# Product 7 of block 0 as seven quarter products in a two-level feed-forward kernel

## The chip, the cores and the metric

The kernel runs on one core of a Trainium2 chip. The metric is the device time of one execution in microseconds (us); the kernel before was given as 337.72 us (median of 3 runs, 337.43 to 338.76). A ratio below is the mean time of one kernel's fast runs over the mean of the other's fast runs of the same rounds on the same chip, so it is not quite the ratio of the medians quoted beside it. It stands with its 95% interval.

The profile names the engines PE (TensorE matmuls), PEld (TensorE weight loads), DVE (VectorE), ACT (ScalarE), POOL (GpSimd) and SP or SPq (SyncE, which issues the transfers here). L978 is line 978 of that kernel's source.

## The reference

```python
def reference(x, w1, b1, w2, b2):          # x: 1 x 2048 x 1024, w1: 1024 x 3584, w2: 3584 x 1024, all bf16
    y = _layernorm(x, axis=-1)
    h = _gelu(jnp.einsum("bsd,df->bsf", y, w1) + b1)
    return jnp.einsum("bsf,fd->bsd", h, w2) + b2
```

## The kernel before

The 2048 rows are two blocks of 1024. In each block the first matmul (L767 and others) makes h, the second multiplies h by w2. The second is split into seven half-size products, numbered 1 to 7 and run in the order 1, 5, 2, 6, 7, 3, 4, whose operands are sums of halves made by VectorE. Each of the seven can be done in two ways. A *plain* product is 4 x 14 matmuls of 512 columns. An *inner* product is split once more, into seven quarter products of 14 matmuls of 256 columns, at the price of further sums (w2 inner sums iT, h inner sums iS) and more evictions. In the kernel before, block 0 does products 6 and 7 plain and the other five inner.

```python
INNER = ((1, 5, 2, 3, 4), SEQ2)          # block 0, block 1
...
def plain(p, a, b, banks_, first, deps):
    for t in range(TH):                  # 4 row tiles
        fn = [(lambda e, k=k, t=t: e.matmul(ps[:, banks_[t].k, :], lhsT=a[0][:, k, t * P:(t + 1) * P],
               rhs=b[0][:, k, :], ...), a[1][k] + b[1][k]) for k in range(NU)]        # NU = 14
...
def inner(p, a, Yo, xb, war, O=None, ...):
    s1 = tt(1, X["21"], X["22"], ALU.add, 5)           # the four h inner sums, VectorE
    s2 = tt(2, s1, X["11"], ALU.subtract, 6)
    s3 = tt(3, X["11"], X["21"], ALU.subtract, 7)
    s4 = tt(4, X["12"], s2, ALU.subtract, 3)
    ...                                                # seven sub-products of 14 matmuls of 256 columns
    sd = copy(lambda: bank_q(c2), lambda: quart(g, 0, 0), (ok[11], subs[1]), ...)      # ScalarE: seed
    k1 = copy(kk_q, lambda: bank_q(c0), (subs[1], *gate), ...)                         # ScalarE: first copy
    k5 = dve(lambda e: plus(e, quart(gt, 1, 1), bank_q(c5), quart(g, 1, 1)), ...)      # VectorE: six evictions
```

Product 7 of block 0 is plain, and the next fetch of w1 for block 1 waits for its second row tile:

```python
M7 = plain(7, S3, B[7], hb, False, [(o,) for o in O12])
w1_use[n - 2] = w1_use[n - 2] + [M7[1]]
```

The layernorm of block 1's tiles runs during block 0's second matmul. Three one-column steps of it are on GpSimd:

```python
vp = add("POOL", 0.2, lambda e: e.tensor_scalar(out=vpe_sb[:, i:i + 1], in0=st_sb[:, i, 0:1],
         scalar1=1.0 / D, scalar2=LN_EPS, op0=ALU.mult, op1=ALU.add), (a2,), ...)
rs = add("POOL", 0.6, lambda e: e.tensor_tensor(out=rstd_sb[:, i:i + 1], in0=vpe_sb[:, i:i + 1],
         in1=nhalf[:, :], op=ALU.pow), (vp, c_nh), ...)
nb = add("POOL", 0.3, lambda e: e.tensor_tensor(out=st_sb[:, i, 1:2], in0=mv_sb[:, i, 1:2],
         in1=rstd_sb[:, i:i + 1], op=ALU.mult), (rs, a1), ...)
```

A planner in the kernel puts every instruction on its engine's list from a table of tuned priorities. On the chip each engine works through its list in order.

## Time and profile before

| | before |
|---|---|
| median time | 337.72 us |
| TensorE busy | 329.3 us, 98%, 2399 matmuls |
| VectorE, ScalarE, GpSimd busy | 281.3, 173.2, 22.5 us |
| moved by DMA | 89.47 MB |

The prediction below shows the page's lines, the timeline, the windows and the one gap. A busy share says little on a pipelined array, so I read TensorE by a ledger. From the timeline every matmul has a start-to-start distance to the next. I subtract its undisturbed pace, 215.8, 109.2 or 55.8 ns for 512, 256 or 128 columns, and sum three things: the paces themselves ("nominal"), the excess before 25 us ("head") and the excess after it ("holes", those over 40 ns). With 1.04 us before the first matmul and 2.81 us from the start of the last to the end this makes up the span: 1.04 + 325.59 + 6.47 + 0.28 + 2.81 = 336.19 of 336.2 us. The only hole is the one before 122 us.

### The profile page before, as it was taken

The numbers are of one execution on the slowest core, as the hardware profiler recorded it, in microseconds if no ns is written. First come the engines' busy times: TensorE is split into PE (matmuls) and PEld (weight loads), VectorE is DVE, ScalarE is ACT, GpSimd is POOL, SyncE is SP. The second block draws the span as 40 slices with busy tenths as digits, with TensorE's granted clock in tenths as the row PEclk, the third lists the DMA queues.
The fourth block names the chain that finished last, engine by engine and source line by source line (L and its number), as shares of the span: only waits on it lengthen the run. The fifth ranks groups of instructions, "written<-read, shape, count | busy, mean of one in ns | idle before, by whom it ended". The sixth has DMA issues, their size and how long they took to land.

```text
span 336.2 us, 6035 instructions
## 1 busy us (share of the span) xinstructions
PE 329.3 (98%) x2399; PEld 223.3 (66%) x2399; DVE 281.3 (84%) x381; ACT 173.2 (52%) x292; POOL 22.5 (7%) x47
## 2 busy tenths in 40 slices
PE   4999999999999999999999999999999999999996
PEld 4977445445468885547875555544545888888885
DVE  3896789998999999979999888886738879999984
ACT  5675978566786687612113666765676521010200
POOL 2420120000020413200000000000000000000000
PEclk9899999999999999999999999999999999999999
DMA  7896999797868999899859549839971999999103
GB/s 269 257 181 182 355 354 321 247 329 262 279 238 305 353 336 361 227 318 379 320 173 328 181 174 336 288 138 292 351 226 50 386 319 367 333 326 311 65 2 125
DMA packets 80310, 89.47 MB, mean 266 GB/s; under 512 B 15130, under 2 KB 67226, under 8 KB 79770
## 3 DMA queue, kind: packets, MB, share of 16 engines
q1 hardware_dynamic: 80138, 88.95, 81.6%
q8 instruction: 19, 0.31, 0.4%
q10 hardware_dynamic: 144, 0.13, 0.1%
q14 instruction: 9, 0.07, 0.1%
HBM read 61.81 MB, written 24.38 MB: 256 GB/s over the span
## 4 chain that ended last, share of the span: by engine, by line
PE 93%; ACT 3%; POOL 1%; DVE 1%; DMA 1%; issue 0%
PE ps L767 42%; PE ps L1063 34%; PE ps L978 7%; PE ps L619 5%; PE ps L692 5%; DMA x_sb<-in_x_dram 1%; POOL st_sb L488 1%; PE ps L504 1%; ACT t_sb L474 1%; ACT t_sb L469 1%; PE ps L1068 0%; ACT sn_sb L962 0%; ACT ps L962 0%; DVE st_sb L418 0%; ACT x_sb L491 0%
## 5 line engine op out<-in xcount | busy, mean ns | idle before, releaser
L767 PE MATMUL ps<-yw_sb,t_sb 128*128 128x512 f16 x336 | 80.0, 379 | 0.0
L767 PE MATMUL ps<-yw_sb,w_sb 128*128 128x512 f16 x312 | 74.7, 379 | 0.0
L792 ACT ACTIVATE h_sb<-ps,b_sb 128x512 f16<-128x512 f32 x78 | 52.9, 686 | 37.0 <-PE ps L767 32.3
L767 PEld LDWEIGHTS ps<-yw_sb,t_sb 128*128 128x128 f16 x336 | 32.8, 98 | 35.8 <-DVE ps L807 0.2
L767 PEld LDWEIGHTS ps<-yw_sb,w_sb 128*128 128x128 bf16 x312 | 30.3, 98 | 33.2 <-ACT ps L780 0.3
L854 DVE TENSOR_TENSOR h_sb<-h_sb 128x2048 f16<-128x2048 f16 (+2 forms) x36 | 38.6, 1084 | 7.3 <-ACT h_sb L792 5.3
L962 ACT COPY sn_sb<-ps 128x512 f32<-128x512 f32 x27 | 15.5, 583 | 32.9 <-DVE o_sb L942 18.2
L1063 PE MATMUL ps<-w2a_sb,h_sb 128*128 128x256 f16 (+1 forms) x252 | 30.3, 273 | 0.0
L942 DVE TENSOR_TENSOR sn_sb<-ps,sn_sb 128x512 f32<-128x512 f32 x35 | 24.0, 687 | 5.3 <-PE ps L1063 4.6
L1063 PEld LDWEIGHTS ps<-w2a_sb,h_sb 128*128 128x128 f16 x252 | 24.7, 98 | 3.9
L942 DVE TENSOR_TENSOR o_sb<-ps,sn_sb 128x512 bf16<-128x512 f32 (+1 forms) x29 | 19.3, 670 | 6.3 <-PE ps L1063 3.7
L978 PE MATMUL ps<-w2a_sb,h_sb 128*128 128x512 f16 x112 | 24.5, 379 | 0.0
L1063 PE MATMUL ps<-w_sb,t_sb 128*128 128x256 f16 x196 | 23.4, 273 | 0.1
L962 ACT COPY ps<-sn_sb 128x512 f32<-128x512 f32 x12 | 7.1, 589 | 30.3 <-PE ps L1063 24.6
L780 ACT COPY ps<-ps 128x512 f32<-128x512 f32 x26 | 14.9, 577 | 14.6 <-PE ps L767 14.5
L1063 PEld LDWEIGHTS ps<-w_sb,t_sb 128*128 128x128 f16 x196 | 19.0, 98 | 2.7 <-ACT sn_sb L962 0.4
L807 DVE TENSOR_TENSOR ps<-ps,sn_sb 128x512 f32<-128x512 f32 x26 | 17.6, 694 | 3.4 <-PE ps L767 3.3
L792 ACT ACTIVATE h_sb<-sn_sb,b_sb 128x512 f16<-128x512 f32 x26 | 18.5, 717 | 3.7 <-DVE sn_sb L821 2.8
L587 DVE TENSOR_TENSOR t_sb<-w_sb,t_sb 128x1024 f16<-128x1024 bf16 x26 | 17.9, 687 | 2.8 <-PE ps L767 1.6
L978 PEld LDWEIGHTS ps<-w2a_sb,h_sb 128*128 128x128 f16 x112 | 11.0, 98 | 12.8
L821 DVE TENSOR_TENSOR sn_sb<-ps,sn_sb 128x512 f32<-128x512 f32 x20 | 13.6, 686 | 5.1 <-PE ps L767 5.0
L619 PE MATMUL ps<-yw_sb,w_sb 128*128 128x128 f16 x256 | 16.7, 226 | 0.4 <-DVE yw_sb L511 0.4
(125 smaller groups left out, 485.4 us busy)
## 6 DMA issues: line engine op xcount, KB each, us to landing
w_sb<-in_w_dram SPq DMA_DIRECT2D x28, 512.0 KB, 5.6
x_sb<-in_w_dram SPq DMA_DIRECT2D x21, 256.0 KB, 6.0
w_sums<-x_sb SPq DMA_DIRECT2D x21, 256.0 KB, 3.5
w2a_sb<-w_inner_sums SPq DMA_DIRECT2D x12, 448.0 KB, 7.3
x_sb<-in_x_dram SPq DMA_DIRECT2D x15, 256.0 KB, 4.3
w_inner_sums<-w_sb SPq DMA_DIRECT2D x4, 896.0 KB, 8.2
x_sb<-w_sums SPq DMA_DIRECT2D x2, 1792.0 KB, 9.1
w_sb<-w_inner_sums SPq DMA_DIRECT2D x8, 448.0 KB, 6.9
```

Of the source, the lines that this page charges most:

```text
L587: return add("DVE", 0.65, lambda e: e.tensor_tensor(out=tv(k), in0=x0, in1=x1, op=ALU.subtract), [*deps, *war.get(k, ())], prio + 0.5 * k, ...
L619: fn = [(lambda e, b=b, hb=hold[f], f=f, k=k, t=t: e.matmul(ps[:, hb.k, t * P:(t + 1) * P], lhsT=lhs[:, k, f * P:(f + 1) * P], rhs=yop[f"A ...
L692: fn = [(lambda e, k=k, v=v: e.matmul(ps[:, bank[r].k, v * QN:(v + 1) * QN], lhsT=xo()[:, k, v * P:(v + 1) * P], rhs=yv()[:, k, :], start= ...
L767: fn = [(lambda e, k=k: e.matmul(ps[:, hold[p].k, :], lhsT=lhs[:, k, :], rhs=yop[yo][:, k, :], start=(first and k == 0), stop=(k == KH - 1 ...
L780: return e.copy(out=dst, in_=src) if o_.eng == "ACT" else e.tensor_copy(dst, src)
L792: r = h_ok[(s, q, u)] = add("ACT", 0.70, lambda e: e.activation(out=dst, in_=src(), func=ACT.Gelu_apprx_tanh, bias=b1_sb[:, f:f + 1], scal ...
L807: o2 = add("DVE", 0.7, lambda e: e.tensor_tensor(out=b5v(b5), in0=b5v(b0), in1=v5(), op=ALU.add), (P6, *o5), pt[7] - SLOT, f"w6_{nm}", all ...
L854: o = add("DVE", cost2(w * dst.shape[-1]), lambda e, k0=k0, k1=k1: e.tensor_tensor(out=dst[:, k0:k1, :], in0=a[0][:, k0:k1, :], in1=b[0][: ...
L942: plus = lambda e, out, x, y: e.tensor_tensor(out=out, in0=x, in1=y, op=ALU.add)
L962: return act(lambda e: e.copy(out=out(), in_=src()), deps, at - 5, name, **k)
L978: fn = [(lambda e, k=k, t=t: e.matmul(ps[:, banks_[t].k, :], lhsT=a[0][:, k, t * P:(t + 1) * P], rhs=b[0][:, k, :], start=(first and k == ...
L1063: fn = [(lambda e, k=k, j=j: e.matmul(ps[:, bank[r].k, j * HI:(j + 1) * HI], lhsT=x[0][:, k, j * P:(j + 1) * P], rhs=y[0][:, k, :], start= ...
```

## The change

The change makes product 7 of block 0 an inner product too. It forms the w2 inner sums of product 7 on the spot, and stores none of them in block 0 (block 1 forms them again in its first stage, as before). The w2 transfers for block 1's product 1 are released one w1 chunk sooner. Two of the layernorm's one-column steps go from GpSimd to ScalarE, the bias transpose goes to the front, and the whole priority table was tuned anew with the overlap of neighbouring VectorE and ScalarE instructions in the plan. A few smaller edits (a queue term in the plan, extra dependencies that keep the order of some sums and transfers) are not shown. Cut to its core:

```diff
-INNER = ((1, 5, 2, 3, 4), SEQ2)
+INNER = ((1, 5, 2, 7, 3, 4), SEQ2)
 ORDER = {...                                    # all entries replaced
+OVL = {"DVE": 0.08, "ACT": 0.09}
...
-            vp = add("POOL", 0.2, lambda e: e.tensor_scalar(... scalar1=1.0 / D, scalar2=LN_EPS ...
+            vp = add("ACT", 0.2, lambda e: e.activation(out=vpe_sb[:, i:i + 1], in_=st_sb[:, i, 0:1], func=ACT.Identity,
+                                                        bias=epsc[:, :], scale=1.0 / D), (a2, c_eps), ...
-            nb = add("POOL", 0.3, lambda e: e.tensor_tensor(out=st_sb[:, i, 1:2], in0=mv_sb[:, i, 1:2],
+            nb = add("ACT", 0.2, lambda e: e.mul(st_sb[:, i, 1:2], mv_sb[:, i, 1:2], rstd_sb[:, i:i + 1]), (rs, a1), ...
...
-                if s + 1 < NSB:
+                if s + 1 < NSB and p != 7:      # product 7: inner sums not stored
                     keep(0, y13, uniq(t1[1][0], t3[1][0]), (5, 7))
...
-                Yo = {1: fetch(1, hold[1], base1[s] + 0.6 * T_MM1, w1_use[n - 3]), ...
+                Yo = {1: fetch(1, hold[1], base1[s] + 0.5 * T_MM1, w1_use[n - 4]), ...
...
-            M7 = plain(7, S3, B[7], hb, False, [(o,) for o in O12])
-            w1_use[n - 2] = w1_use[n - 2] + [M7[1]]
-            ...                                  # four evictions o22, four copies O3
+            gw, okq, sub7 = inner(7, S3, inner_sums(7, B[7], Y0, war_of(sub2, 2)), X0, war_of(sub2),
+                                  O=(gu, {11: U[1], 12: U[1], 21: U[3], 22: U[3]}), kk=x_sb[:, NT - 1, :].bitcast(F32))
+            w1_use[n - 2] = w1_use[n - 2] + [sub7[5]] + flat(S4)
+            Yo3 = inner_sums(3, B[3], [two(xf), *halves(xf)[3:1:-1]], {}, True)      # product 3's sums into the x buffer
```

## The prediction

> **What bounds the kernel now.** I read four views in this order: the page, TensorE's timeline, the windows by stage, and the timeline around the one gap that TensorE has. The page first (part 1: busy us, share, instructions; part 4: the chain that ended last):
>
> ```profile
> PE 329.3 (98%) x2399; PEld 223.3 (66%) x2399; DVE 281.3 (84%) x381; ACT 173.2 (52%) x292; POOL 22.5 (7%) x47
> ...
> PE 93%; ACT 3%; POOL 1%; DVE 1%; DMA 1%; issue 0%
> ```
>
> TensorE is 98% busy and carries 93% of the chain. Busy time alone proves little, since matmuls overlap, so the pace has to be checked. TensorE's timeline over products 2, 6 and 7 of block 0 (start, length, what):
>
> ```profile
> 126.56 6.21 PE L978 MATMUL ps<-w2a_sb,h_sb 128*128 128x512 f16 x28
> 132.60 1.69 PE L1063 MATMUL ps<-w_sb,h_sb 128*128 128x256 f16 x14
> 134.13 1.69 PE L1063 MATMUL ps<-yw_sb,t_sb 128*128 128x256 bf16 x14
> 135.66 18.29 PE L978 MATMUL ps<-w2a_sb,h_sb 128*128 128x512 f16 x84
> 153.79 1.69 PE L1063 MATMUL ps<-w2a_sb,h_sb 128*128 128x256 bf16 x14
> ```
>
> L978 is a plain product, L1063 an inner one. From start to start, 28 wide matmuls take 132.60 - 126.56 = 6.04 us, 215.7 ns each; 14 narrow ones 134.13 - 132.60 = 1.53 us, 109.3 ns each. The 112 matmuls of L978 are products 6 and 7; 56 of the 84 in the fourth line are product 7. The same reading over the whole timeline finds TensorE at this pace, without a hole, from about 11 us until its last matmul begins at 333.4 us; the only exception is 0.28 us just before 122 us. So the span is the sum of TensorE's matmuls plus a head and a tail.
>
> What could break that is VectorE. Windows by stage (stretch, its length, then busy us and instructions by engine):
>
> ```profile
> 97.00:126.00 29.00, 28.88 (x257) 24.81 (x256) 26.70 (x28) 20.84 (x36) 6.37 (x8) 1.00 0.95 307
> 126.50:153.80 27.30, 27.30 (x144) 13.77 (x142) 24.91 (x30) 12.69 (x22) 5.05 (x9) 1.00 1.01 305
> 153.80:178.80 25.00, 25.00 (x214) 20.85 (x213) 23.40 (x27) 3.92 (x7) 0.00 (x0) 1.00 0.79 280
> 178.80:200.00 21.20, 21.20 (x112) 10.75 (x110) 18.06 (x32) 12.43 (x21) 0.00 (x0) 1.00 0.68 241
> 200.00:258.00 58.00, 58.00 (x305) 29.66 (x304) 41.68 (x59) 38.33 (x64) 0.00 (x0) 1.00 0.72 237
> ```
>
> The third busy number is VectorE. Around product 7 it has only 27.30 - 24.91 = 2.4, then 25.00 - 23.40 = 1.6, then 21.20 - 18.06 = 3.1 us free; from 200 us on it has 16.3 us free. The gap before 122 us (POOL, ACT, the weight load that waits):
>
> ```profile
> 113.97 2.82 POOL L488 TENSOR_TENSOR st_sb<-mv_sb,rstd_sb 128x1 f32<-128x1 f32 x1
> ...
> 116.83 1.24 ACT L491 ACTIVATE x_sb<-x_sb,st_sb,rstd_sb 128x1024 f16<-128x1024 bf16 x1 [2.00 <-POOL st_sb L488]
> 117.98 0.56 ACT L962 COPY sn_sb<-ps 128x512 f32<-128x512 f32 x1
> ...
> 121.96 1.42 PEld L1063 LDWEIGHTS ps<-w_sb,t_sb 128*128 128x128 f16 x14 [0.40 <-ACT sn_sb L962]
> ```
>
> A one-column multiplication took 2.82 us on GpSimd, ACT stood 2.00 us for it in its order, its bank copies came late, and TensorE paid 0.28 us.
>
> **What the Trainium skill says.** "TensorE: Matmul & The Clock Gate", section "Back-to-back issue gap", gives N/2.4 + 2.5 ns for a single warm matmul, 215.8 at N=512 and 109.2 at N=256; the trace's 215.7 and 109.3 agree. The same section calls this too high for streams with weight loads and gives some 131 ns at N=512; this trace does not show that. "VectorE: DVE Perf Modes", section "The perf-mode tier table", has tensor_tensor at 2x on 16-bit SBUF data and at 1x with a PSUM operand. The trace agrees: 1,792 fp16 elements in 1,086 ns (0.61 ns each), 512 fp32 elements with PSUM in 687 ns (1.34 ns each). "SBUF — State Buffer", section "Who interferes with whom", says that a VectorE instruction with two SBUF inputs keeps out a GpSimd one that reads SBUF. L488's eight runs of the same operation lasted 191 to 2,823 ns, which fits that.
>
> **The change part by part.**
>
> TensorE. Product 7 of block 0 loses 56 matmuls at 215.7 ns = 12.08 us and gains 7 sub-products of 14 at 109.3 ns = 10.71 us. That is -1.37 us, all on the path, since TensorE has no holes there.
>
> VectorE, with the step from start to start where instructions follow each other (the timeline shows 1.93 us for 3,584 fp16 elements, 1.00 for 1,792, 0.60 for a 128x512 eviction; the 128x1024 fp32 sum is taken as 1.15 us, its 1.225 less the same overlap). Added: the w2 inner sums 1.93 + 2 x 1.00 = 3.93; the four h inner sums 4.00; six evictions 3.60; two row sums 2.30; together 13.8. Removed: four evictions of the plain product, 2.4. Net +11.4 us. It is not on the path by itself, but it falls where 2.4 + 1.6 + 3.1 = 7.1 us are free.
>
> ACT. Four copies (O3) go and four come (U); seed and first copy of product 7 add 2 x 0.58 us. The two one-column steps of the second layernorm move here from GpSimd, 8 x 2 x 0.2 = 3.2 us by L472's 200 ns. ACT has 14.6 us free in the second window above and 21.1 in the third, so this costs nothing. What it buys is the 0.28 us gap, since ACT no longer stands behind L488; the power on GpSimd (0.55 us) stays.
>
> DMA. Product 7 stores no sums in block 0, and block 1 forms them during its first matmul stage as before, so the traffic stays near 89.5 MB. Product 3's sums move into the x buffer, so they must follow block 1's transposes out of it, and product 7's first copy goes into the place of x tile 7. The earlier fetch of block 1's product 1 moves a transfer for which TensorE does not wait now: nothing.
>
> Head. The bias transpose may slide into TensorE's idle time before 6.8 us; it holds the array 0.13 us now (9.64 to 9.77). I count -0.1.
>
> Sum without any new wait: 337.72 - 1.37 - 0.28 - 0.1 = 335.97 us.
>
> **The rivals.** First, VectorE becomes the bound of the stage. An inner product costs it 3.93 + 4.00 + 3.60 = 11.5 us against 10.7 us on TensorE, so three in a row (7, 3, 4) run it behind, and the plain product 7, which it used to get ahead, is gone. For: 11.4 us more into 7.1 us free leaves 4.3 us to be pushed past 200 us. Against: from there 16.3 us are free, block 1's sums for products 6 and 7 (8.2 us, L1370) can be done later, and TensorE already mixes first-stage products with the end of product 4. If none of the overhang is hidden it is 340.3 us; if half is, 338.1.
>
> Second, a new wait on the transposes. In the trace before, SyncE issues transposes from 103 to 147 us, one landing a median of 5.0 us after issue, and half of those for tiles 4 to 7 must follow the end of product 2 (about 135.7 us). Product 7 would begin near 141.7 and want its first copy by about 144; a transpose of tile 7 issued third after 135.7 at some 1.7 us each lands near 146. That would be up to 2 us of TensorE wait, unless product 2 is brought to an end earlier, which the reordering may do. Alone: 336 to 338 us.
>
> Third, all is hidden: the whole order was tuned anew, with the overlap of VectorE's instructions now in the plan. 336.0 us.
>
> **Range and chances.** I take the third as most likely, with an allowance of 0.6 us for small waits of the first two kinds: 335.97 + 0.6 = 336.6 us. The low end, 335.5, is the clean sum less a noise of 0.5 (the three runs before spread 1.3 us); the high end, 338.8, is the first rival with a third of the overhang hidden and no more. Over 2% faster means under 331.0 us, which would need over 5 us that no part offers: 0.01. Over 2% slower means over 344.5 us, twice the whole overhang: 0.02. Within 2%: 0.97.
>
> **What would show it right or wrong.** Right: L978 at 56 matmuls and L1063 98 more; VectorE's busy time near 281.3 + 11.4 = 292.7 us; no wait on L488; TensorE still at 215.7 and 109.3 ns without holes from 11 us on. Wrong by the first rival: weight loads of L1063 or L767 waiting for VectorE between 140 and 215 us, VectorE without idle there. Wrong by the second: a hole early in product 7 that ends with the first copy on ACT, which waited for a transpose. The prediction fails upward if those holes add to more than 2 us, and downward if the head shrinks by a microsecond, which I do not expect.

## The result, and the profile after

The kernel after took 337.97 us (median of 5, 337.88 to 339.0), the kernel before in the same rounds 338.5 us (median of 5, 337.43 to 338.87): ratio 0.9998, interval 0.9974 to 1.0022. The time lies inside the forecast range, but the forecast said a gain of 1.1 us over 337.72, and none was measured. The page of the kernel after, parts 1 and 4:

```profile
PE 328.9 (98%) x2441; PEld 227.0 (68%) x2441; DVE 290.5 (86%) x392; ACT 178.1 (53%) x310; POOL 17.2 (5%) x32
...
PE 89%; DMA 7%; DVE 3%; SPq 1%; issue 0%; POOL 0%
```

There are 42 more matmuls (98 - 56) and 9.2 us more on VectorE. In the chain ScalarE and GpSimd are gone, and transfers and VectorE have come in. TensorE's timeline over products 6 and 7 (start, length, what):

```profile
131.61 1.69 PE L1086 MATMUL ps<-w_sb,h_sb 128*128 128x256 f16 x14
133.14 9.23 PE L1000 MATMUL ps<-w2a_sb,h_sb 128*128 128x512 f16 x42
142.21 1.69 PE L1086 MATMUL ps<-w2a_sb,h_sb 128*128 128x256 f16 x14
143.74 3.22 PE L1086 MATMUL ps<-w_sb,t_sb 128*128 128x256 f16 x28
...
157.91 1.90 PE L786 MATMUL ps<-yw_sb,w_sb 128*128 128x512 f16 x8 [0.25 <-DMA w_sb<-in_w_dram]
```

The pace is what it was: 14 narrow matmuls in 143.74 - 142.21 = 1.53 us. After product 6 product 7 starts without a hole. The last line shows two things: block 1's first-stage products (L786) now start at 157.9 us inside the second stage of block 0, where the timeline of before has the first of them at 172.13 us, and this one waits for a transfer. ScalarE around the old gap:

```profile
119.41 1.21 ACT L984 COPY ps<-sn_sb 128x512 f32<-128x512 f32 x2
120.55 0.29 ACT L502 ACTIVATE st_sb<-mv_sb,rstd_sb 128x1 f32<-128x1 f32 x1
```

The one-column step takes 0.29 us here and nobody waits for GpSimd; the gap before 122 us is gone. The windows by stage, in the columns of the prediction's table:

```profile
97.00:126.00 29.00, 29.00 (x256) 24.85 (x255) 28.59 (x31) 27.15 (x52) 4.63 (x3) 1.00 0.99 326
126.50:153.80 27.30, 27.30 (x198) 19.12 (x197) 27.24 (x31) 14.09 (x25) 3.12 (x3) 1.00 0.94 292
153.80:178.80 25.00, 24.75 (x202) 19.40 (x200) 24.97 (x30) 4.72 (x9) 0.00 (x0) 1.00 1.07 336
178.80:200.00 21.20, 21.17 (x119) 11.23 (x118) 19.13 (x31) 11.39 (x19) 0.00 (x0) 1.00 0.51 180
```

From 97 to 178.8 us VectorE, the third busy number, has 0.4, 0.06 and 0.03 us free. In these four windows and the next (45.14 against 41.68) it does 10.3 us more than before. TensorE has holes now. Each stands here with the line that causes it: first the one at 41 us with VectorE's lines before it, then the weight fetch for the one at 158 us, then the weight loads that waited at 183 and 194 us:

```profile
40.96 1.25 PE L786 MATMUL ps<-yw_sb,t_sb 128*128 128x512 f16 x5 [0.29 <-DVE sn_sb L804]
...
37.14 0.69 DVE L595 TENSOR_TENSOR t_sb<-w_sb 128x1024 f16<-128x1024 bf16 x1 [0.91 <-DMA w_sb<-in_w_dram]
...
39.62 0.68 DVE L1434 TENSOR_TENSOR dl_sb<-b_sb 128x512 f32<-128x512 bf16 x1
40.22 0.68 DVE L804 TENSOR_TENSOR sn_sb<-ps,sn_sb 128x512 f32<-128x512 f32 x1
...
147.50 0.94 SPq L362 DMA_DIRECT2D w_sb<-in_w_dram  x2
...
183.55 1.41 PEld L786 LDWEIGHTS ps<-yw_sb,t_sb 128*128 128x128 f16 x8 [0.52 <-DVE t_sb L605]
...
194.08 0.79 PEld L711 LDWEIGHTS ps<-sn_sb 128*128 128x128 f16 x8 [0.27 <-DVE sn_sb L667]
```

At 41 us VectorE had stood 0.91 us for w1 chunk 3, then did its list in order, a bias step (L1434) ahead of the sum (L804) that TensorE wanted. At 158 us the weights had been asked for only at 147.50, after the last h sum of product 3 had ended at 146.96, and landed at 157.86. At 183 and 194 us VectorE is simply not yet there. "TensorE: Matmul & The Clock Gate", section "Architectural detail: the array is 16× 32×32, not 1× 128×128", says in the Trainium skill that VectorE and ScalarE take their instructions strictly first in, first out; the trace agrees, the sum of L804 did not pass the waiting one. So an order is as good as a dependency.

The ledger of the two kernels, the repeats included that are told below:

| kernel, profile | nominal | head | holes (where) | span |
|---|---|---|---|---|
| before | 325.59 | 6.47 | 0.28 (122) | 336.20 |
| before, again | 325.59 | 6.64 | 1.52 (115, 198) | 337.62 |
| after | 324.21 | 6.80 | 1.21 (41, 158, 183, 194) | 336.13 |
| after, again | 324.21 | 8.43 | 1.17 (43, 159, 185, 196) | 337.71 |
| after, third | 324.21 | 7.21 | 1.39 (41, 158, 184, 195) | 336.71 |

The nominal sum fell by 325.59 - 324.21 = 1.38 us. In the means of these profiles the holes give back 1.26 - 0.90 = 0.36 and the head 7.48 - 6.56 = 0.92 us. Together that is -0.10 us, and the mean spans differ by -0.06. So the saved matmul time is there, and the question is what holes and head have to do with the change.

### The profile page after: what moved, and what is told of

Its sections match the earlier page's. It is cut to its first block, busy times and chain, and to the rows that moved or that the text cites. A ratio compares the mean times of both kernels' runs of the same rounds, so it can differ in the third digit from the quotient of the medians.

```text
span 336.1 us, 6135 instructions
## 1 busy us (share of the span) xinstructions
PE 328.9 (98%) x2441; PEld 227.0 (68%) x2441; DVE 290.5 (86%) x392; ACT 178.1 (53%) x310; POOL 17.2 (5%) x32
## 2 busy tenths in 40 slices
DMA packets 80278, 89.47 MB, mean 266 GB/s; under 512 B 15098, under 2 KB 67194, under 8 KB 79738
## 4 chain that ended last, share of the span: by engine, by line
PE 89%; DMA 7%; DVE 3%; SPq 1%; issue 0%; POOL 0%
PE ps L786 39%; PE ps L1086 37%; DMA w_sb<-in_w_dram 5%; PE ps L711 5%; PE ps L638 4%; PE ps L1000 4%; DMA x_sb<-in_x_dram 2%; SPq L362 1%; PE ps L518 1%; PE ps L1091 0%; DVE sn_sb L964 0%; DVE st_sb L431 0%; DVE sn_sb L804 0%; DVE h_sb L873 0%; DVE t_sb L595 0%
## 5 line engine op out<-in xcount | busy, mean ns | idle before, releaser
L786 PE MATMUL ps<-yw_sb,t_sb 128*128 128x512 f16 x336 | 80.2, 379 | 0.3 <-DVE sn_sb L804 0.3
L786 PE MATMUL ps<-yw_sb,w_sb 128*128 128x512 f16 x312 | 75.8, 379 | 0.3 <-DMA w_sb<-in_w_dram 0.3
L786 PEld LDWEIGHTS ps<-yw_sb,t_sb 128*128 128x128 f16 x336 | 32.7, 98 | 36.8 <-DVE sn_sb L804 1.0
L786 PEld LDWEIGHTS ps<-yw_sb,w_sb 128*128 128x128 bf16 x312 | 30.2, 98 | 32.7 <-ACT ps L799 0.6
L1086 PE MATMUL ps<-w2a_sb,h_sb 128*128 128x256 f16 (+1 forms) x280 | 33.3, 273 | 0.0
L1086 PEld LDWEIGHTS ps<-w2a_sb,h_sb 128*128 128x128 f16 x280 | 27.4, 98 | 4.0
L964 DVE TENSOR_TENSOR sn_sb<-ps,sn_sb 128x512 f32<-128x512 f32 x40 | 27.2, 686 | 1.6 <-PE ps L1086 1.5
L964 DVE TENSOR_TENSOR o_sb<-ps,sn_sb 128x512 bf16<-128x512 f32 (+1 forms) x25 | 16.6, 666 | 6.1 <-ACT ps L1162 2.9
L873 DVE TENSOR_TENSOR t_sb<-h_sb 128x1792 f16<-128x1792 f16 x16 | 17.3, 1086 | 0.8 <-ACT h_sb L811 0.6
L840 DVE TENSOR_TENSOR sn_sb<-ps,sn_sb 128x512 f32<-128x512 f32 x20 | 13.6, 687 | 4.4 <-PE ps L786 4.4
L638 PEld LDWEIGHTS ps<-yw_sb,w_sb 128*128 128x128 bf16 x256 | 15.5, 101 | 1.7 <-DMA w_sb<-in_w_dram 1.0
```

The costliest lines, as they stand in the source:

```text
L638: fn = [(lambda e, b=b, hb=hold[f], f=f, k=k, t=t: e.matmul(ps[:, hb.k, t * P:(t + 1) * P], lhsT=lhs[:, k, f * P:(f + 1) * P], rhs=yop[f"A ...
L786: fn = [(lambda e, k=k: e.matmul(ps[:, hold[p].k, :], lhsT=lhs[:, k, :], rhs=yop[yo][:, k, :], start=(first and k == 0), stop=(k == KH - 1 ...
L840: c22 = add("DVE", 0.69, lambda e: e.tensor_tensor(out=v5(), in0=b5v(b0), in1=v5(), op=ALU.add), (P7, o2), pt[4] - SLOT, f"c7_{nm}")
L873: o = add("DVE", cost2(w * dst.shape[-1]), lambda e, k0=k0, k1=k1: e.tensor_tensor(out=dst[:, k0:k1, :], in0=a[0][:, k0:k1, :], in1=b[0][: ...
L964: plus = lambda e, out, x, y: e.tensor_tensor(out=out, in0=x, in1=y, op=ALU.add)
L1086: fn = [(lambda e, k=k, j=j: e.matmul(ps[:, bank[r].k, j * HI:(j + 1) * HI], lhsT=x[0][:, k, j * P:(j + 1) * P], rhs=y[0][:, k, :], start= ...
```

## The experiments

The theory at the outset: VectorE's list, full from 97 to 194 us, leaves TensorE waiting in four places, and these holes ate the gain. The rival: noise of the head hides a gain that is there, and the holes have causes unlike each other. In all edits `move(engine, name, to)` takes one instruction out of an engine's finished list and puts it ahead of another (`after=True`: behind it); nothing else changes unless shown.

### The kernel after once more

> The changed kernel once more, for the spread of its TensorE holes. If they belong to the order of its instructions, the trace shows again about 0.45 us near 41 us, 0.4 us near 158 us, 0.2 us near 183.5 us and 0.15 us near 194 us, each within 0.1 us. If they come from the luck of transfers, at least the two that wait for a w1 or x transfer (the head, 158 us) differ by 0.3 us or more or are gone. Time: same as the kernel before within 0.3%.

338.11 us (337.52 to 341.31, 6 runs), ratio 0.9999 (0.9965 to 1.0034). The holes are at the same places with the same sizes (table above); the head is 1.6 us longer than the first time. So the three late holes look like properties of the kernel and the head does not. For the one near 41 us, later runs show that it depends on when a transfer lands.

### Three single changes to the kernel after

bias_late:

```diff
+        move("DVE", "dl", "c7_0_3", after=True)    # L1434 behind the sum of L804
```

> The changed kernel with one swap in VectorE's order: the sum that releases product 4 of unit 3 (c7_0_3) goes ahead of the 0.68 us bias difference (dl). If the hole near 41 us is only that queueing, it goes from 0.45 to under 0.1 us, the rest of the trace shifts 0.4 us earlier, and the time falls by 0.4 us (ratio to the changed kernel 0.9988). If something else bounds TensorE, the hole's time comes back as wider holes later and the span stays at 336.1 us.

The hole at 41 us went; another came at 68 us, from the same kind of cause (VectorE in line behind a weight sum whose transfer had landed late):

```profile
68.24 1.04 PE L786 MATMUL ps<-yw_sb,w_sb 128*128 128x512 f16 x4 [0.33 <-DVE ps L826]
```

The holes are 1.36 us in sum, the time 338.06 us, ratio 0.9986 (0.9965 to 1.0007).

The swap did close the hole: less the head excess of its profile, the first half of w1 chunk 3 landed at 30.3 us here (36.70 - 6.38), as late as in the three profiles of the kernel after (37.12 - 6.80, 38.71 - 8.43, 37.48 - 7.21), which have holes of 0.40 to 0.45 us. But an early landing does the same: at 29.9 us in w1_early the hole is 0.09 us, and at 29.4 us in dve_minus there is none, though neither edit touches this part; in dve_minus there is none at 68 us either. So neither hole is a fixed cost.

w1_early:

```diff
+        o = named["w1_1_0_0"]                       # first half of block 1's first weight chunk
+        o.deps = [d for d in o.deps if d.name != "M75_0" and not d.name.startswith("hS4_0")]
+        move("SP", "w1_1_0_0", "w2_0_B22_0")
```

> The changed kernel with the first half of block 1's first w1 chunk no longer held back for the h sums S4 and for sub-product 5 of product 7, and issued before the two B22 loads (near 140 us in place of 147.5 us). If the hole near 158 us is the late landing of this transfer, it goes from 0.42 us to under 0.05 us and the span falls by 0.4 us. If VectorE is what bounds there, the time returns in wider holes near 183 and 194 us and the span stays.

The fetch went out at 140.66 us in place of 147.50, and the hole at 158 us is gone. But a hole of 0.33 us came five microseconds later, where ScalarE's seed of product 4 is late:

```profile
158.10 1.89 PE L786 MATMUL ps<-yw_sb,w_sb 128*128 128x512 f16 x8
...
163.41 1.70 PE L1086 MATMUL ps<-h_sb 128*128 128x256 f16 x14 [0.17 <-ACT ps L984]
```

The holes at 183 and 194 us did not change (0.19 and 0.15 us), against the rival. Holes 0.82 us, time 338.64 us, ratio 1.0012 (0.998 to 1.0043).

dve_minus, a wrong result (relative error 0.028):

```diff
+        for k, name in enumerate(("iS5_7_0_0", "iS6_7_0_0", "iS7_7_0_0", "iS3_7_0_0")):
+            named[name].fn = lambda e, k=k: e.tensor_tensor(out=tiny[:, k:k + 1], in0=nhalf[:, :], in1=nhalf[:, :],
+                                                            op=ALU.subtract)     # one column each, in place of 1792
```

> Wrong result on purpose: the four h inner sums of product 7 in block 0 (1.0 us each on VectorE) are replaced by one-column operations, so VectorE has 3.7 us less to do between 137 and 149 us. If VectorE's saturation makes the three late holes, S4 ends earlier, w1 is issued some 1 to 3 us earlier, and the holes near 158, 183.5 and 194 us (0.76 us together) all but vanish: span down by 0.6 to 0.8 us, the hole near 41 us unchanged. If they come from transfers or from TensorE's order alone, they stay.

With four of product 7's sums taken away the late holes stayed: 0.47, 0.19 and 0.15 us at 158, 183 and 194. Ratio 0.9988 (0.9963 to 1.0013). VectorE's windows, in the columns of the tables above:

```profile
126.50:153.80 27.30, 27.30 (x198) 19.11 (x196) 23.95 (x32) 14.02 (x25) 1.38 (x2) 1.00 0.95 282
153.80:178.80 25.00, 24.70 (x200) 19.27 (x199) 24.95 (x29) 5.05 (x9) 0.00 (x0) 1.00 1.06 337
```

In the first window VectorE does 3.3 us less (23.95 against 27.24), and spent it, up to 148 us, in waits for ScalarE and TensorE; the fetch of w1 moved only from 147.50 to 146.91 us. In the second it is as full as before. So work taken away ahead of 148 us does not close the late holes. Whether less work after 148 us would, this run does not test.

### The kernel before once more, and one part of the change alone

> The kernel before once more, unchanged, for the noise of the old side. Theory (the saved matmul time is given back in two ways: reproducible holes of TensorE that the old kernel does not have, and a head before 25 us that varies by some 2 us from execution to execution whatever the kernel): the ratio is 1.000 within 0.3%; the profile has the hole of 0.28 us at 122 us again and no hole at 158, 183 or 194 us; its head excess may lie anywhere between 6.3 and 8.5 us. Rival (the old kernel has the same holes at times and its first profile was lucky): holes of over 0.15 us show up between 150 and 200 us here as well.

338.54 us (337.87 to 339.34), ratio 0.9984 (0.9958 to 1.0009). Half the expectation was wrong: the gap before 122 us was absent, and the old kernel had two others:

```profile
115.40 1.70 PE L1063 MATMUL ps<-w2a_sb,t_sb 128*128 128x256 f16 x14 [1.03 <-ACT sn_sb L962]
...
112.22 1.06 ACT L469 ACTIVATE t_sb<-x_sb 128x1024 f16<-128x1024 bf16 x1 [2.22 <-DMA x_sb<-in_x_dram]
...
198.21 1.90 PE L767 MATMUL ps<-yw_sb,t_sb 128*128 128x512 f16 x8 [0.17 <-DVE ps L807]
```

ScalarE stood 2.22 us for an x tile and did its layernorm passes before the copy that TensorE wanted. So the old kernel too pays, in some executions, 1.2 us when a transfer lands late. The other hole, at 196 to 198 us, recurs in four of the six profiles of the kernel before and its variants (0.16 to 0.33 us). The first profile, on which I built, was a quiet one. The ratio is a measure of the noise as well: here a kernel against itself gave 0.9984.

before_ln_act takes only the layernorm's part of the change:

```diff
+        for i in range(NT):                          # vpe1_i and nb1_i from GpSimd's list to ScalarE's
+            vp.fn = lambda e, i=i: e.activation(out=vpe_sb[:, i:i + 1], in_=st_sb[:, i, 0:1], func=ACT.Identity,
+                                                bias=epsc[:, :], scale=1.0 / D)
+            nb.fn = lambda e, i=i: e.mul(st_sb[:, i, 1:2], mv_sb[:, i, 1:2], rstd_sb[:, i:i + 1])
+            ...                                     # epsc set once on GpSimd; both moved into ScalarE's list
```

> The kernel before with one part of the change alone: the two one-column steps of the second layernorm on ScalarE in place of GpSimd, the orders otherwise as they were. Theory of the prediction: the hole at 122 us (0.28 us) goes and nothing else moves, sum of the matmul times 325.59 us as before, holes 0 to 0.1 us; in time 0.3 us, which lies under the noise, so ratio 0.997 to 1.001 and only the trace can tell. Rival (the hole comes from the power on GpSimd, which stays there): a wait of ScalarE on GpSimd's power of about the same length remains and the hole stays at 0.2 us or more.

The gap is gone, with all else as in the kernel before:

```profile
118.16 4.75 PE L1065 MATMUL ps<-w_sb,t_sb 128*128 128x256 f16 x42
122.75 1.47 PE L1065 MATMUL ps<-o_sb,h_sb 128*128 128x256 f16 x12
```

Forty-two matmuls run through from 118.16 to 122.75. Ratio 0.9974 (0.9951 to 0.9997), three times the 0.28 us of the gap, so I repeated it:

> The kernel before with only the one-column steps of the second layernorm on ScalarE, once more. Theory (worth its gap of 0.28 us and no more; the rest of the first result was noise): ratio 0.998 to 1.000, no hole at 122 us, head excess anywhere between 6.0 and 7.0 us. Rival (it is worth 0.9 us): ratio 0.996 to 0.998 again.

0.9984 (0.9964 to 1.0004). In this profile the x tile was late again: it made its hole of 1.15 us at 115 us, and since ScalarE was still behind after it, one of 0.14 us before 122.6 us. So with x tiles in time the gap before 122 us goes when ScalarE no longer stands behind GpSimd's multiplication, and a late x tile makes its holes with or without this part. What the part is worth in time is some tenths of a microsecond, up to 0.9 by the first result, and is not settled better than that.

### First attempts to close all holes at once

late_closed and all_closed are the early fetch of w1_early with more moves:

```diff
+        move("PE", "M46_0", "M42_0")                       # late_closed and all_closed: two sub-products of product 4
+        move("DVE", "yS3_1_0", "w1T2_1_0", after=True)
+        move("DVE", "yi13_1", "w1T3_1_2")
+        move("DVE", "dl", "c7_0_3", after=True)            # all_closed alone, with the next four
+        move("SP", "w1_0_3_0", "pw0_2")
+        move("SP", "w1_0_3_1", "pw0_2")
+        move("SP", "w1_0_5_0", "pw2_1")
+        move("SP", "w1_0_5_1", "pw2_1")
```

> The same without the three edits for block 0's first stage (w1 chunks 3 and 5, bias copy): only those for the holes at 158, 183 and 194 us. Theory: the three holes (together 0.76 us) are gone, under 0.15 us is left between 150 and 200 us; the hole at 41 us or 68 us may be there or not, 0 to 0.5 us, as it follows the landing of a weight transfer. Rival: holes of 0.7 us or more remain between 150 and 215 us at other places.

> The kernel after with only orders changed, each for one hole that its traces showed: w1 chunks 3 and 5 of block 0 issued ahead of the second product's preparation, chunk 0 of block 1 issued about 7 us sooner, the bias copy ahead of a left-over on VectorE, a weight sum and an input sum moved behind what TensorE waits for, and two sub-products of product 4 exchanged. Theory (the holes are what ate the gain, and each is a matter of order): the holes of 1.2 us fall to under 0.3 us, the sum of the matmul times stays 324.2 us, so that span minus head is 1.0 us shorter than the after kernel's, and ratio 0.995 to 0.998. Rival (VectorE is the bound of the stage from 97 to 194 us, and an order only moves the hole): new holes elsewhere between 150 and 215 us with a sum of 0.7 us or more, ratio 0.998 to 1.001.

Both misses. late_closed: 341.36 us (one run, state unknown), holes 5.08 us, over half of them (1.80 and 0.95) from the two exchanged sub-products, one of which now wanted a sum that VectorE makes later. all_closed: 348.13 us, ratio 1.0273 (1.0251 to 1.0296), holes 11.5 us with the slow matmuls counted in. Its worst hole:

```profile
67.72 3.60 PE L786 MATMUL ps<-yw_sb,t_sb 128*128 128x512 f16 x8 [4.57 <-DVE sn_sb L840]
71.11 1.91 PE L786 MATMUL ps<-yw_sb,w_sb 128*128 128x512 f16 x4
```

The fetch of chunk 5 must wait for its buffer until 57.6 us. Put ahead of the w2 loads on SyncE, which issues in order, it held them back; VectorE waited for them till 65.6 us and TensorE for VectorE 4.57 us. Then (71.11 - 67.72) / 8 = 0.42 us per matmul, twice the pace: the array had gone to its slow clock (granted clock 0.50 from 68 to 73 us) and stayed there for some 5.5 us, which cost 2.7 us more. The Trainium skill has this in "TensorE: Matmul & The Clock Gate", section "Part 1: The HAM clock gate": after about 3.4 us of idleness the array falls to half its clock, and the window of the measure runs freely. This trace agrees.

### A replay, and a small set of moves

To stop guessing I replayed the trace: each instruction keeps its measured duration, each transfer its measured time to landing, each semaphore its measured delay (in the trace of the kernel after a median of 0.035 us from VectorE to ScalarE, 0.058 to TensorE), and only the lists change. On the profiles of the kernel after this gave the four holes back to within 0.02 us by my account. With it I looked for single exchanges that shorten the sum.

```diff
+        o = named["w1_1_0_0"]
+        o.deps = [d for d in o.deps if d.name != "M75_0" and not d.name.startswith("hS4_0")]
+        move("SP", "w1_1_0_0", "w2_0_B22_1", after=True)
+        move("DVE", "dl", "c7_0_3", after=True)
+        move("DVE", "w1T1_0_5", "w1T2_0_4", after=True)
+        move("DVE", "k2_4_0", "k5_4_0", after=True)
+        move("DVE", "o21_3_0", "w1T2_1_0", after=True)
+        move("DVE", "w1T1_1_1", "w1T2_1_2")
+        move("DVE", "c7_1_0", "w1T4_1_1")
+        move("DVE", "gS3_5g_1_1", "yi2_1", after=True)
+        move("DVE", "w1T3_1_2", "yi2_1", after=True)
```

> The kernel after with ten small moves in the orders, found by replaying the measured durations and waits of its traces with the orders exchanged, after the two rough attempts had opened new waits: chunk 0 of block 1's weights issued behind the second half of B22's load instead of behind the last h sum, and nine exchanges of neighbours on VectorE; no instruction is added or removed. Theory (VectorE is full from 97 to 194 us but its order is what leaves TensorE waiting): the holes at 41, 68, 158, 183 and 194 us are gone, one of 0.32 us is left at 162 to 164 us (ScalarE's seed of product 4's accumulation), the sum of the matmul times stays 324.2 us, so the span less the head excess is 0.9 us shorter than the after kernel's; ratio 0.995 to 0.998. Rival (VectorE's sum of work bounds, orders can't help): holes of 0.8 us or more remain and the ratio is 0.998 to 1.001.

337.71 us, ratio 0.9978 (0.9962 to 0.9994), holes 0.50 us: 0.18 left at 41 us and the expected one at 162:

```profile
157.12 1.89 PE L786 MATMUL ps<-yw_sb,w_sb 128*128 128x512 f16 x8
...
162.43 1.70 PE L1086 MATMUL ps<-h_sb 128*128 128x256 f16 x14 [0.16 <-ACT ps L984]
...
182.04 3.62 PE L786 MATMUL ps<-yw_sb,t_sb 128*128 128x512 f16 x16
```

Nothing waits at 158, nor at 183, where sixteen matmuls run through. The unchanged kernel after:

> The kernel after, unchanged, beside the others on one chip. Theory: holes again at 158, 183 and 194 us with 0.75 us together, and 0.4 us at 41 or 0.5 us at 68 us; ratio 0.998 to 1.001. Rival: if the holes are chance, they lie elsewhere or are absent.

338.98 us, ratio 1.0015 (1.0001 to 1.003), the four holes in place, 1.39 us. The mean of the reordered kernel is 337.61 - 338.98 = -1.37 us against it, of which its profile shows 1.39 - 0.50 = 0.89 us as closed holes and 0.50 us as a shorter head. The repeat:

> The re-ordered kernel after once more, unchanged. Holes after 25 us 0.3 to 0.5 us; ratio 0.996 to 0.999 as the first time (0.9978).

337.56 us, ratio 0.9975 (0.9941 to 1.0009), holes 0.44 us. Both results were correct. The same instructions in another order gain 0.22 and 0.25% where 0.33% was forecast; the interval of the repeat still touches 1, and the holes, not the times alone, tell where the gain comes from. The hole near 41 us is smaller (0.18 and 0.11 us) but not gone.

### A dose of VectorE's work in both kernels

The four h inner sums of product 7 (kernel after) or of product 3 (kernel before), which VectorE makes in the same stretch, are computed twice:

```diff
+        for r in (5, 6, 7, 3):
+            o = named[f"iS{r}_7_0_0"]                # before_dve_plus: f"iS{r}_3_0_0"
+            twin = Op("DVE", o.cost, o.fn, o.deps, o.prio, o.name + "_twin")
+            order["DVE"].insert(order["DVE"].index(o), twin)
+            ...                                      # the original follows its twin
```

> The kernel after with the four h inner sums of product 7 computed twice, 4.0 us more of VectorE's work between 138 and 152 us, result unchanged. Theory (the change has used up VectorE's slack in this stretch, so each further microsecond is TensorE's): 4.0 us longer, new holes at about 145 (1.9 us), 152 (1.0 us), 158 (0.8 us) and 166 us (0.6 us). Rival (VectorE still has room before 200 us, the holes are single accidents): under 1.5 us longer.

> The kernel before with the same dose, the four h inner sums of product 3 computed twice, 4.0 us more on VectorE in the same stretch. Theory (before, VectorE had some microseconds to spare here): 1.4 us longer, holes at 156 (0.6 us) and 160 us (0.8 us), so 2.6 us of the 4.0 are hidden. Rival (no slack before either): 4 us longer.

TensorE's timeline of the kernel after with the dose:

```profile
146.69 3.37 PE L1086 MATMUL ps<-w_sb,t_sb 128*128 128x256 f16 x28 [1.97 <-DVE w_sb L1044]
...
154.03 1.69 PE L1086 MATMUL ps<-w2a_sb,t_sb 128*128 128x256 f16 x14 [0.91 <-DVE t_sb L873]
...
159.34 1.70 PE L1086 MATMUL ps<-w_sb,h_sb 128*128 128x256 f16 x14 [0.56 <-DVE sn_sb L964]
```

and of the kernel before with it:

```profile
156.35 1.70 PE L1063 MATMUL ps<-w_sb,t_sb 128*128 128x256 f16 x14 [0.81 <-DVE w_sb L854]
...
160.26 1.70 PE L1063 MATMUL ps<-w_sb,t_sb 128*128 128x256 f16 x14 [0.67 <-ACT sn_sb L962]
```

After: holes 5.50 us, 4.1 more than the kernel after (1.39); 344.03 us, ratio 1.0174 (1.0139 to 1.021). Before: 2.16 us, 1.9 more than in its first profile (0.28); 340.29 us, ratio 1.0058 (1.004 to 1.0077). Without leaning on that one profile: the two new holes at 156 and 160 us are 1.8 us together. So by the holes the dose of 4.0 us is paid in full after the change and about half before it. In the mean times it is 5.4 us (344.38 - 338.98) and 2.0 us; two of the four dosed runs of the kernel after are 2 to 3.5 us longer than the profiled one, which no trace explains. So before the change VectorE had some 2 us to spare ahead of product 3's sums, and after it none ahead of product 7's.

### The head

Left over was the head. Two kernels carry the old head's order into the new kernel, one the new into the old:

```diff
+        move("SP", "w1_0_0_1", "b1", after=True)     # after_head, and reordered_head with the ten moves
+        move("PE", "b1t", "plain_0_0_30", after=True)
+        move("PE", "T0_1_0", "b1t", after=True)
+        move("PE", "T0_1_1", "T0_1_0", after=True)
+        move("DVE", "y0_1", "st0_2_0", after=True)
```

> The kernel after with the head's order as in the kernel before: the second half of the first weight chunk is fetched after x tile 3 and the bias, and TensorE transposes the bias and tile 1 ahead of the matmuls that need that half. Theory A (the new head costs 0.7 us, because its matmuls wait for the second half of the weights and the array stays at its slow clock longer): head excess 6.0 to 6.7 us, ratio 0.997 to 0.999. Theory B (chance of the clock and of the transfers): head excess anywhere between 6.3 and 8.4 us, ratio 0.999 to 1.002 as the kernel after has it. The holes after 25 us stay 1.2 to 1.4 us in either case.

> The kernel before with the head's order of the kernel after, nothing else. Theory A: head excess about 7.1 us, 0.7 us longer, ratio 1.001 to 1.003. Theory B: no difference, head excess 6.0 to 6.7 us, ratio 0.999 to 1.001.

> Both together: the ten moves that close the holes and the old head. Theory A: another 0.7 us off the re-ordered kernel, ratio 0.994 to 0.997, the shortest of all. Theory B: the same as the re-ordered kernel, 0.996 to 0.999.

| kernel | head in its profile | ratio |
|---|---|---|
| after_head | 6.83 us | 0.9994 (0.9974 to 1.0013) |
| before_head_after | 6.36 us | 1.0018 (0.9996 to 1.004) |
| reordered_head | 7.45 us | 0.9966 (0.994 to 0.9991) |

The times lean to theory A, each by half a thousandth to two thousandths against its partner (after 0.9998 to 1.0015, before 1, reordered 0.9975), and none does so clearly. The heads of the profiles point both ways. Over all profiles the old order of the head has 6.57 us on average (7 profiles, 6.0 to 7.5), the new 7.08 us (12 profiles, 6.4 to 8.4): 0.5 us with an uncertainty as large. This stays open. Sorted by kernel instead, the six profiles of the kernel before and its variants average 6.36 us (6.0 to 6.6), the 13 of the kernel after and its variants 7.15 us (6.4 to 8.4), whichever head order they have. So in the profiles it is not the exchanged order that parts them; what does, or whether it is chance, stays open. In the longest head, TensorE's timeline and then the windows of 5 us, whose last numbers are the granted clock, the DMA share and GB/s:

```profile
10.13 1.46 PE L638 MATMUL ps<-yw_sb,w_sb 128*128 128x128 f16 x12 [0.22 <-DMA w_sb<-in_w_dram]
...
5.00:10.00 5.00, 2.50 (x24) 2.07 (x24) 2.57 (x7) 2.52 (x6) 1.29 (x3) 0.75 0.99 327
10.00:15.00 5.00, 4.87 (x51) 4.65 (x52) 3.98 (x10) 3.25 (x6) 1.77 (x4) 0.57 0.98 334
```

TensorE waits for the second half of the first weight chunk, and the clock between 10 and 15 us is 0.57 of full speed. The slow clock lasts until some 14 us here and until about 10 us in the shortest head (before_ln_act); 72 matmuls run at twice their pace before 25 us here, 50 there. The clock is not all: in reordered_head (7.45 us) they are only 45, and the rest of its excess is waiting. reordered_head also met the late w1 chunk 3 again, 0.66 us at 42 us, and so it is not clearly better than reordered.

## Why the prediction was right or wrong

**Right.** The TensorE step: forecast -1.37, measured -1.38 us. This is counts times pace; that the pace held shows in what the ledger leaves over, under 0.1 us in each profile of the two kernels. The ScalarE step: the gap before 122 us, forecast -0.28, is gone from every profile of the kernel after. before_ln_act removed it by this part alone. The second rival, a wait of product 7 for the transposes, did not occur. The traffic stayed at 89.47 MB.

**Mis-sized.** VectorE's added work: forecast 11.4 us, measured 10.3 in the windows from 97 to 258 us and 9.2 in the whole page. The instructions themselves last 12.3 us longer in sum (312.6 against 300.3); the page counts the overlap of neighbours once, and 22.1 us overlap in place of 19.0, because more of them follow each other directly. The first rival had the right mechanism in part: VectorE is full, and work was pushed past 200 us (45.14 us there in place of 41.68, 3.5 more where 4.3 were forecast). But TensorE hardly paid for it; the holes after 150 us are 0.76 us in the first profile. The timeline shows block 1's first-stage products in TensorE's time from 157.9 us on; that they hid the overflow is my reading and was not tested.

**Wrong, and this is the step that failed:** "I take the third as most likely, with an allowance of 0.6 us for small waits of the first two kinds". The waits measured 1.2 to 1.4 us. None is of the second kind. Two, at 183 and 194 us (0.34 us together), bear the sign that was named for the first kind, a weight load that waits for a full VectorE; but the amount of work does not fix them, since the same work in another order has no hole there. The other two come from weight transfers that land late: at 41 us, outside the stage that I had looked at, onto a VectorE with a bias step in front, and at 158 us because the fetch had to wait for the last h sum. Re-ordering, with the hold on that one fetch lifted, closed 0.7 to 0.9 us of these waits without removing any work. I had read that VectorE would be full, and asked only how much would overflow, not what stands ahead of what.

**Also wrong, and perhaps as large:** the head, "I count -0.1". It was 6.8 to 8.4 us in the three profiles of the new kernel against 6.5 and 6.6 in the two of the old, 0.9 us longer in the mean. The runs with exchanged orders do not settle why, and the cause stays open. And the base: 337.72 us was a low sample. The old kernel's medians in the six later timings were 338.4 to 338.7 us, and its first profile had the smaller hole sum of the two.

So the 1.38 us of saved matmul time was there and was given back to waits and head. Between the two first profiles the waits take 0.93 us of it (1.21 - 0.28) and the head 0.33; in the means of the five profiles it is 0.36 and 0.92. How it divides depends on which execution of the old kernel is taken, as its own holes were 0.28 us in one and 1.52 in the other. What is shown by experiment is the part of the waits: closing 0.7 to 0.9 us of them took the ratio from 0.9998, 0.9999 and 1.0015 to 0.9978 and 0.9975. The prediction missed the ratio by 0.3% (336.6 / 337.72 = 0.9967 against 0.9998).

## What to carry to other kernels

When a change takes work from the bound engine and gives it to one that is nearly full, do not ask only whether the sum still fits: a full engine with a fixed order can pass a late transfer on, as at 41 us here, so read for each wait what stands ahead of the instruction that is wanted. Test the slack with a dose of dummy work in both kernels; here 4 us opened holes of 4.1 us after the change and 1.9 us before it. And profile the old kernel more than once before a gain of half a percent is forecast from it, since its own holes moved by more than a microsecond.

## What the Trainium skill lacked or had wrong

- "TensorE: Matmul & The Clock Gate", section "Back-to-back issue gap": it has about 131 ns for a 512-column matmul in a stream with weight loads; here, with one weight load to every matmul (2441 of each), it is 215.8 ns at 512 columns and 109.2 at 256 over the whole kernel, which is its formula for the single matmul.
- The same page, section "Part 1: The HAM clock gate", counts the warm-up as under 1% of a span and not worth fitting. In the shortest head 50 slow matmuls of 128 columns cost some 51 ns each more, 2.5 us (0.8%), in the longest 72 cost 3.7 us (1.1%). At that size it is still not to be passed over: the head, with the waits for the first transfers, took 6.0 to 8.4 us, and its spread of 2.4 us (0.7%) between profiles is more than the 0.4% that was at stake here.
- The same page, section "HAM oscillation — how this bites in real kernels", prices the fall to half clock on a kernel that falls at every tile. Of a single gap the runs show: 4.57 us of idleness cost 2.7 us more in slow matmuls, over the 5.5 us that followed.
- "SBUF — State Buffer", section "Who interferes with whom", has no times for a one-column GpSimd instruction that is kept out; here the same multiplication took 191 to 2,823 ns, and the longest (113.97 to 116.79 us) outlasted two VectorE instructions that followed each other directly (113.73 to 115.74 and 115.66 to 116.74 us), ending 0.05 us after the second.
- "DMA: Bandwidth & Descriptors" has no figure for how much the landing of one transfer varies between executions; over twelve profiles with the new head order the second half of the first weight chunk, asked for at the same 2.7 us, landed between 8.2 and 10.1 us.
